# Start of a linear-attention and GEGLU kernel: fills of two load buffers moved ahead, first batch's casts, kv, x and norms regrouped by head pairs, first two gate tiles run by rows of x

## The chip, the cores and the metric

The kernel runs on one core of a Trainium2 chip. The metric is the device time of one execution in microseconds (us). The page of a profile counts from the first to the last record of the core; that span is some 2 us shorter than the time of the same execution. Where a difference matters the number of runs and a standard error stand beside it.

## The reference, cut to what matters

```python
# q, k, v: 8 batches x 8 heads x 576 rows x 64, f32; moe_w_*: 512 x 1536 (out: 1536 x 512)
q_s = softmax(q, axis=-1)                       # over the 64 columns of a head
k_s = softmax(k, axis=2)                        # over the 576 rows
kv  = einsum('bhsd,bhse->bhde', k_s, v)         # 64 x 64 for each head
x   = einsum('bhsd,bhde->bhse', q_s, kv)        # -> (4608, 512) rows
out = (gelu(x @ w_gate) * (x @ w_val)) @ w_out
```

## The kernel before

All large work is matmuls in f16. Two heads share the 128 rows of a weight tile ("a head pair", `hp` 0 to 3; "a group" is two pairs). PSUM is the memory that matmuls write to. `xt` holds x transposed; "row i of x" is the part of it that comes from head pair i. "A gate tile" is 128 of the 1536 columns of w_gate and w_val: four matmuls for each of the two (`psg` and `psv`), one for each row of x. Before the first gate matmul the first batch has to go through: load q, exponential on ScalarE, row sums, reciprocal and multiply on VectorE or GpSimd, transposes on TensorE (to `eqt`); load k, exponential; load v, cast to f16; kv on TensorE, its norm on VectorE (`kv_sb`); x on TensorE, copied to f16 (`xt`). While TensorE has nothing to do it multiplies a tile of zeros (`warm_pe`, the warm-ups); in the profile before, these matmuls start 0.43 us apart at first and 0.22 us apart later.

```python
    for nm, n, fill in (("k", 2, -1e30), ("v", 1, 0.0), ("q", 2, 0.0)):   # after the other memsets
        for i in range(n):
            t = const.tile([P, H, NC * D], f32, name=f"{nm}t{i}")
            (nc.vector if i == 0 else nc.gpsimd).memset(t[:, :, 0:D], fill)
    ...
    def norm_sum(b, hp, n0=0):         # one head pair
        ...
        nc.vector.reduce_sum(rq, e, axis=mybir.AxisListType.X)
        nc.vector.reciprocal(out=rrq, in_=rq)
    def norm_mul(b, hp, eng="dve"):    # VectorE, or GpSimd with eng="pool"
        ...
    def unit_kv(b, g):                 # two head pairs in one PSUM tile
        pskv = ps_att.tile([P, 2, 2 * VW], f32, name="pskv", tag="att")
        for j in range(2): ...         # 5 matmuls each
        nc.vector.reciprocal(out=rck, in_=pskv[:, :, D])
        for j in range(2): ...         # kv_sb = pskv * rck * mask
    ...
    exp("q", 0, 0, 4, 1); exp("q", 0, 4, 8, 1); exp("k", 0, 0, 4); exp("k", 0, 4, 8)
    warm_pe(35)
    norm(0, 0, "dve", 1);  norm(0, 1, "pool", 1)
    norm(0, 2, "dve", 1);  norm(0, 3, "pool", 1)
    unit_t(0, 0, "dve")                # transposes of pairs 0, 1, and the copy to eqt
    warm_pe(9)
    cast_v(0, 0, 4, "dve")             # heads 0-3 in one instruction
    cast_v(0, 4, 6, "act")
    unit_t(0, 1, "act")
    cast_v(0, 6, 8, "dve")
    ...
    warm_pe(2)
    unit_kv(0, 0)
    unit_kv(0, 1)
    unit_x(0, 0, "act", True);  unit_x(0, 1, "act", True)
    unit_x(0, 2, "dve", True);  unit_x(0, 3, "act", True)
    ...
    # ffn_first: psg, psv of gate tile 0 with rows 0, 1 of x, then of tile 1,
    # then row 2 of both, then row 3 of both
```

The softmax here doesn't subtract the row's maximum and nothing guards it: scores larger than these inputs give would overflow.

Of the kernel before, what the change touches and what calls it, by code (L numbers as in the profile page):

```python
# [9 lines left out]
f32 = mybir.dt.float32  # L10
# [8 lines left out]
def kernel(  # L19
# [44 lines left out]
    warm = const.tile([P, 512], f16)  # L64
    nc.vector.memset(warm, 0.0)
    ident = const.tile([P, P], f16)
    make_identity(nc, ident)
    mask = const.tile([P, 2, D], f32)
    nc.vector.memset(mask, 0.0)
    nc.vector.memset(mask[0:64, 0, :], 1.0)  # L70
    nc.vector.memset(mask[64:128, 1, :], 1.0)
    tiny = const.tile([P, 80], f32)
    nc.vector.memset(tiny, 0.0)
    ek_b, eq_b, v16_b = [], [], []
    for i in range(2):
        ek_b.append(const.tile([P, NC, C], f16, name=f"ek{i}"))
        eq_b.append(const.tile([P, NC, C], f16, name=f"eq{i}"))
        v16_i = const.tile([P, NC, H, VW + 1], f16, name=f"v16_{i}")
        nc.gpsimd.memset(v16_i[:, :, :, D:D + 1], 1.0)
        v16_b.append(v16_i)  # L80
    xtr = const.tile([P, HP, B * REM], f16)
    q0r = const.tile([64, H, D], f32)
    eq0r = const.tile([P, C], f16)
    nc.vector.memset(eq0r[64:128, :], 1.0)

    ld_b = {}
    for nm, n, fill in (("k", 2, -1e30), ("v", 1, 0.0), ("q", 2, 0.0)):
        ld_b[nm] = []
        for i in range(n):
            t = const.tile([P, H, NC * D], f32, name=f"{nm}t{i}")  # L90
            (nc.vector if i == 0 else nc.gpsimd).memset(t[:, :, 0:D], fill)
            ld_b[nm].append(t)

# [67 lines left out]
    def norm_sum(b, hp, n0=0):  # L161
# [6 lines left out]
        st[(b, "norm", hp)] = (e, rrq, n)  # L168

    def norm_mul(b, hp, eng="dve"):  # L170
        e, rrq, n = st[(b, "norm", hp)]
        (nc.gpsimd if eng == "pool" else nc.vector).tensor_tensor(  # L172
            out=e, in0=e, in1=rrq.unsqueeze(-1).to_broadcast((P, n, 2, D)), op=ALU.mult)
# [19 lines left out]

    def unit_kv(b, g):
        pskv = ps_att.tile([P, 2, 2 * VW], f32, name="pskv", tag="att")
        for j in range(2):
            hp = 2 * g + j
            for n in range(NC):
                nc.tensor.matmul(  # L199
                    pskv[:, j, :], ek_b[b % 2][:, n, hp * P:(hp + 1) * P],  # L200
                    v16_b[b % 2][:, n, 2 * hp:2 * hp + 2, 0:VW],
                    start=(n == 0), stop=(n == NC - 1))
        rck = att.tile([P, 2], f32, name="rck", tag="rck")
        nc.vector.reciprocal(out=rck, in_=pskv[:, :, D])
        for j in range(2):
            kv_sb = att.tile([P, 2, D], f16, name="kv_sb", tag="kv", bufs=12)
            nc.vector.scalar_tensor_tensor(  # L207
                out=kv_sb,
                in0=pskv[:, j, :].rearrange("p (h e) -> p h e", e=VW)[:, :, 0:D],
                scalar=rck[:, j:j + 1], in1=mask, op0=ALU.mult, op1=ALU.mult)  # L210
            st[(b, "kv", 2 * g + j)] = kv_sb

    def get_eqt(b):
# [5 lines left out]
    def unit_t(b, g, eng="dve"):  # L219
        eqt = get_eqt(b)  # L220
        pst = ps_att.tile([P, 2, MAIN], f16, name="pst", tag="att")
        for j in range(2):
            hp = 2 * g + j
            for n in range(NM):
                nc.tensor.transpose(  # L225
                    pst[:, j, n * P:(n + 1) * P],
                    eq_b[b % 2][:, n + 1, hp * P:(hp + 1) * P], ident)
        copy_on(eng, eqt[:, 2 * g:2 * g + 2, 0:MAIN], pst)

# [56 lines left out]
    def unit_xrem(b, eng="act"):  # L286
# [4 lines left out]
        copy_on(eng, xtr[:, :, b * REM:(b + 1) * REM], psx)  # L291

    def warm_pe(n):
        ps = ps_big.tile([P, 512], f32, name="pswarm", tag="mm")
        for _ in range(n):
            nc.tensor.matmul(ps, ident, warm, start=True, stop=True)  # L296
# [25 lines left out]
    def ffn_first(xt, after):  # L322
# [14 lines left out]
        for fi, (psg, psv) in enumerate(ps):  # L337
            mm_gv(psg, wg_sb, xt, fi, [3])
            mm_gv(psv, wv_sb, xt, fi, [3])
            hts.append(gate(psg, psv))  # L340
        return hts

# [80 lines left out]
    exp("k", 0, 4, 8)  # L423
    warm_pe(35)
    norm(0, 0, "dve", 1)
    norm(0, 1, "pool", 1)
    norm(0, 2, "dve", 1)
    norm(0, 3, "pool", 1)
    unit_t(0, 0, "dve")
    warm_pe(9)  # L430
    cast_v(0, 0, 4, "dve")
    cast_v(0, 4, 6, "act")
    unit_t(0, 1, "act")
    cast_v(0, 6, 8, "dve")
    for h0 in (0, 4):
# [4 lines left out]
    warm_pe(2)  # L440
    unit_kv(0, 0)
    unit_kv(0, 1)
    cast_w("wg", 0, "pool")
    cast_w("wv", 0, "pool")
    unit_x(0, 0, "act", True)
    unit_x(0, 1, "act", True)
    unit_x(0, 2, "dve", True)
    unit_x(0, 3, "act", True)
    preload(ACTF.Gelu)
# [10 lines left out]
    def at(b, kind, i, *fns):  # L460
# [3 lines left out]

    at(0, FI, NFI - 1, L(exp, "q", 1), L(exp, "k", 1, 0, 4),
       L(cast_w_o, 3), L(cast_w_o, 4), L(cast_w_o, 5),
       L(norm, 1, 0), L(norm, 1, 1, "pool"), L(norm_sum, 1, 2), L(norm_mul, 1, 2, "pool"),
       L(cast_v, 1, 0, 4, "act"), L(exp, "k", 1, 4, 8))
# [6 lines left out]
              [L(unit_x, 1, 3, "dve")]]  # L475
    first = {0: [[], []], 1: first1}

# [53 lines left out]
    for b in order:  # L531
        xt = get_xt(b) if b < B else xtr
        hts = []
        fi0 = 0
        if b in first:
            hts = ffn_first(xt, first[b])
            fi0 = len(hts)
            ride(b, FI, fi0 - 1)
# [57 lines left out]
```

## Time and profile before

| | before |
|---|---|
| median of the runs before the prediction | 321.93 us (3 runs, 321.76 to 321.95) |
| span of the profiled execution | 319.8 us |
| TensorE busy | 314.4 us (98%) |
| q of the first batch lands (ScalarE's first exponential) | 6.44 us |
| k, v land | 10.07, 13.03 us |
| first kv matmul | 14.60 us |
| third gate tile starts | 20.78 us |

How to read it: TensorE is the bound, and it runs without a gap from the first gate tiles to the end except for a few short waits. The landing of a load is read here as the start of the first ScalarE instruction that needs it. The chain of waits gives a first kv matmul at 14.66 where the timeline has 14.60, since the chain cuts at the end of the matmul before; I use the timeline.

### The profile page before, as it was taken

Reading aid. Unit: us, or ns where it says so; the run is one execution under the profiler, and the core shown is the slowest. Engines: PE = TensorE matmul, PEld = TensorE weight load, DVE = VectorE, ACT = ScalarE, POOL = GpSimd, SP = SyncE. Lnnn points to the kernel's source line nnn. Section 1 sums busy time; section 2 is a strip of 40 time slices with the busy share of each in tenths; the row PEclk is TensorE's granted clock in tenths of the full one; section 3 lists DMA queues with packets and bytes.
Section 4 is the critical chain, followed back from the end, with each engine's and each line's share of the span. In section 5 each row is a group of like instructions: output and inputs, shape, how many; then the busy total and the mean of one; then the engine's idle time right before and its main releaser. Section 6 shows DMA issues by size and latency. Waiting matters only on the chain.

```text
span 319.8 us, 4482 instructions
## 1 busy us (share of the span) xinstructions
PE 314.4 (98%) x1650; PEld 149.5 (47%) x1650; DVE 194.7 (61%) x343; ACT 140.0 (44%) x178; POOL 44.5 (14%) x60
## 2 busy tenths in 40 slices
PE   8999999999999999999999999999999999999995
PEld 3544454445445444544444444444444444444443
DVE  3944366498889578846794679457952444233431
ACT  3563564898352563246423743384321233103300
POOL 2567460340002000120003000300000000000000
PEclk9999999999999999999999999999999999999999
DMA  6999999940187216821492039302011110040002
GB/s 230 367 383 395 400 389 385 394 148 0 68 291 250 54 66 210 321 62 66 124 383 81 29 124 373 121 21 119 14 55 29 68 66 0 16 108 10 0 34 99
DMA packets 42342, 50.76 MB, mean 159 GB/s; under 512 B 3408, under 2 KB 38096, under 8 KB 42320
## 3 DMA queue, kind: packets, MB, share of 16 engines
q1 hardware_dynamic: 42176, 50.41, 45.6%
q8 instruction: 13, 0.21, 0.3%
q14 instruction: 9, 0.07, 0.1%
q10 hardware_dynamic: 144, 0.07, 0.1%
HBM read 37.75 MB, written 9.44 MB: 148 GB/s over the span
## 4 chain that ended last, share of the span: by engine, by line
PE 96%; ACT 1%; issue 1%; DVE 1%; POOL 0%; POOLq 0%; ACTq 0%
PE psg L304 28%; PE psy L348 28%; PE psv L304 28%; PE pswarm L296 4%; PE pskv L199 3%; PE psx L282 2%; PE pst L225 1%; PE psl L369 1%; DVE kv_sb L207 0%; ACT L309 0%; ACT L148 0%; PE psxr L289 0%; ACT eq L148 0%; PE pstr L237 0%; ACT gl L309 0%
## 5 line engine op out<-in xcount | busy, mean ns | idle before, releaser
L309 ACT ACTIVATE gl<-psg 128x512 f32<-128x512 f32 x108 | 63.9, 598 | 127.3 <-PE psg L304 125.5
L311 DVE SCALAR_TENSOR_TENSOR ht<-psv,gl 128x512 f16<-128x512 f32 x108 | 72.9, 682 | 64.7 <-PE psv L304 63.2
L304 PE MATMUL psg<-xt,wg_sb 128*128 128x512 f16 x384 | 100.6, 379 | 0.2
L304 PE MATMUL psv<-xt,wv_sb 128*128 128x512 f16 x384 | 100.2, 379 | 0.0
L348 PE MATMUL psy<-wo_sb,ht 128*128 128x512 f16 x420 | 95.5, 379 | 0.0
L304 PEld LDWEIGHTS <-wv_sb 128*128 128x128 f16 x432 | 42.2, 98 | 51.5 <-issue 0.9
L304 PEld LDWEIGHTS <-wg_sb 128*128 128x128 f16 x432 | 41.5, 98 | 47.6 <-issue 0.8
L348 PEld LDWEIGHTS <-ht 128*128 128x128 f16 x420 | 40.4, 98 | 47.2 <-DVE ht L311 0.2
L397 DVE TENSOR_SCALAR yo<-psy 128x512 f32<-128x512 f32 x30 | 20.6, 689 | 31.0 <-PE psy L348 31.0
L126 POOL CAST v<-vt 128x640 f16<-128x640 f32 x26 | 18.3, 743 | 140.1 <-DMA vt<-in_v_dram 122.9
L165 DVE TENSOR_REDUCE rq<-eq 128x10 f32<-128x640 f16 (+1 forms) x32 | 25.4, 792 | 9.3 <-ACT eq L148 8.9
L172 DVE TENSOR_TENSOR eq<-eq,rrq 128x640 f16<-128x640 f16 (+1 forms) x28 | 22.9, 817 | 0.3
L148 ACT ACTIVATE ek<-kt 128x1280 f16<-128x1280 f32 (+1 forms) x11 | 19.1, 1746 | 3.0 <-DVE rrq L167 1.6
L148 ACT ACTIVATE eq<-qt 128x2560 f16<-128x2560 f32 (+1 forms) x9 | 18.3, 2049 | 4.3 <-DMA qt<-in_q_dram 4.2
L248 DVE STREAM_TRANSPOSE et<-eq 128x640 f16<-128x640 f16 x20 | 16.9, 845 | 0.7
L128 ACT CAST xt<-psx 128x512 f16<-128x512 f32 x17 | 9.2, 588 | 15.9 <-PE psx L282 15.9
L296 PE MATMUL pswarm<-warm,ident 128*128 128x512 f16 x46 | 12.3, 430 | 1.4 <-POOL ident masks.py:199 1.4
L304 PE MATMUL psg<-xtr,wg_sb 128*128 128x512 f16 x48 | 12.3, 379 | 0.0
L304 PE MATMUL psv<-xtr,wv_sb 128*128 128x512 f16 x48 | 12.3, 379 | 0.0
L199 PEld LDWEIGHTS <-ek 128*128 128x128 f16 x160 | 10.3, 97 | 3.6 <-issue 0.4
L199 PE MATMUL pskv<-v,ek 128*128 128x130 f16 x160 | 11.8, 220 | 0.0
L130 DVE CAST xt<-psx 128x512 f16<-128x512 f32 x15 | 9.7, 682 | 1.8 <-PE psx L282 1.8
(59 smaller groups left out, 129.4 us busy)
## 6 DMA issues: line engine op xcount, KB each, us to landing
out_dram<-yo SPq DMA_DIRECT2D x14, 512.0 KB, 3.5
qt<-in_q_dram SPq DMA_DIRECT2D x9, 512.0 KB, 6.7
kt<-in_k_dram SPq DMA_DIRECT2D x7, 640.0 KB, 7.4
vt<-in_v_dram SPq DMA_DIRECT2D x7, 640.0 KB, 7.9
qt<-in_q_dram SPq DMA_DIRECT2D x7, 640.0 KB, 6.1
kt<-in_k_dram SPq DMA_DIRECT2D x7, 512.0 KB, 8.0
vt<-in_v_dram SPq DMA_DIRECT2D x7, 512.0 KB, 8.5
eqt<-et SPq DMA_DIRECT2D x80, 40.0 KB, 1.9
```

The lines of the kernel that those rows point to most:

```text
L126: nc.gpsimd.tensor_copy(out=dst, in_=src)
L148: nc.scalar.activation(out=dst[:, n0:NC, h0 * D:h1 * D].rearrange("p n (h d) -> p h n d", d=D), in_=tiles[(nm, b)][:, h0:h1, n0 * D:NC * D ...
L165: nc.vector.reduce_sum(rq, e, axis=mybir.AxisListType.X)
L172: (nc.gpsimd if eng == "pool" else nc.vector).tensor_tensor(out=e, in0=e, in1=rrq.unsqueeze(-1).to_broadcast((P, n, 2, D)), op=ALU.mult)
L199: nc.tensor.matmul(pskv[:, j, :], ek_b[b % 2][:, n, hp * P:(hp + 1) * P], v16_b[b % 2][:, n, 2 * hp:2 * hp + 2, 0:VW], start=(n == 0), sto ...
L248: nc.vector.transpose(out=et[:, :, hp].rearrange("p c (n i) -> p n c i", i=32), in_=eq_b[b % 2][:, :, hp * P:(hp + 1) * P].rearrange("p n ...
L296: nc.tensor.matmul(ps, ident, warm, start=True, stop=True)
L304: nc.tensor.matmul(ps, w[:, ci, fi * P:(fi + 1) * P], xt[:, ci, :], start=(ci == 0), stop=(ci == HP - 1))
L309: nc.scalar.activation(out=gl, in_=psg, func=ACTF.Gelu)
L311: nc.vector.scalar_tensor_tensor(out=ht, in0=psv, scalar=_H_SCALE, in1=gl, op0=ALU.mult, op1=ALU.mult)
L348: nc.tensor.matmul(psy, hts[fi][:, ns * P:(ns + 1) * P], wo_sb[:, fi, :], start=(fi == 0), stop=(fi == NFI - 1))
L397: nc.vector.tensor_scalar(out=yo, in0=psy, scalar1=1.0 / _H_SCALE, scalar2=None, op0=ALU.mult)
```

## The change

The intent is to shorten the stretch up to 20.78 us. It puts the fills of k's and v's load buffers ahead of the other memsets, so that the load of k can be issued sooner; sums the rows of q for two head pairs with one instruction and gives one more multiply to VectorE; drops two warm-ups; casts v by head pair on two engines; does kv of heads 0 to 3 first and x of those heads before the rest; and runs the first two gate tiles row of x by row of x, with x of the upper heads in between. In the second batch, q's exponential is split and one multiply moves from GpSimd to VectorE.

```diff
     nc.vector.memset(warm, 0.0)
+    nc.vector.memset(ld_b["k"][0][:, :, 0:D], -1e30)      # fills of the load buffers: before, the last memsets
+    nc.vector.memset(ld_b["v"][0][:, :, 0:D], 0.0)
     nc.vector.memset(tiny, 0.0)
     nc.vector.memset(mask, 0.0)
 ... (cut: tiles are allocated earlier, the same memsets follow; norm_pair, kv_mm, kv_norm are new functions)
-    warm_pe(35)
-    norm(0, 0, "dve", 1)
-    norm(0, 1, "pool", 1)
-    norm(0, 2, "dve", 1)
-    norm(0, 3, "pool", 1)
-    unit_t(0, 0, "dve")
+    norm_pair(0, 0, 1, ("dve", "dve"))
+    warm_pe(33)
+    unit_t(0, 0, None)
+    evac_t0 = st["evac_t"]
+    norm_pair(0, 1, 1, ("dve", "pool"))
+    evac_t0("dve")
     warm_pe(9)
-    cast_v(0, 0, 4, "dve")
+    unit_t(0, 1, None)
+    cast_v(0, 0, 2, "dve")
+    cast_v(0, 2, 4, "act")
+    cast_v(0, 6, 8, "dve")
     cast_v(0, 4, 6, "act")
-    unit_t(0, 1, "act")
-    cast_v(0, 6, 8, "dve")
 ... (cut: loads)
     warm_pe(2)
-    unit_kv(0, 0)
-    unit_kv(0, 1)
+    kv_mm(0, 0, 0)
+    kv_mm(0, 0, 1)
+    kv_norm(0, 0)
+    kv_mm(0, 1, 1)
     unit_x(0, 0, "act", True)
+    kv_mm(0, 1, 0)
     unit_x(0, 1, "act", True)
-    unit_x(0, 2, "dve", True)
-    unit_x(0, 3, "act", True)
+    st["evac_t"]("dve")
+    kv_norm(0, 1)
 ... (cut: ffn_first0, for batch 0 alone)
+        go(0, (0, 1))          # gate tile 0, rows 0 and 1 of x: psg, psv of a row, then of the next
+        xs()                   # x of pairs 2 and 3
+        go(1, (0, 1))
+        go(0, (2,))
+        go(1, (2,))            # then row 3 of tile 0, its gelu; row 3 of tile 1, its gelu
 ... (cut)
-    at(0, FI, NFI - 1, L(exp, "q", 1), L(exp, "k", 1, 0, 4),
+    at(0, FI, NFI - 1, L(exp, "q", 1, 0, 4), L(exp, "q", 1, 4, 8), L(exp, "k", 1, 0, 4),
-       L(norm, 1, 0), L(norm, 1, 1, "pool"), L(norm_sum, 1, 2), L(norm_mul, 1, 2, "pool"),
+       L(norm, 1, 0), L(norm, 1, 1), L(norm_sum, 1, 2), L(norm_mul, 1, 2, "pool"),
```

More of the change, by code (lines that the diff above doesn't have):

```diff
@@ L64 @@
     warm = const.tile([P, 512], f16)
-    nc.vector.memset(warm, 0.0)
     ident = const.tile([P, P], f16)
-    make_identity(nc, ident)
     mask = const.tile([P, 2, D], f32)
-    nc.vector.memset(mask, 0.0)
-    nc.vector.memset(mask[0:64, 0, :], 1.0)
-    nc.vector.memset(mask[64:128, 1, :], 1.0)
     tiny = const.tile([P, 80], f32)
-    nc.vector.memset(tiny, 0.0)
     ek_b, eq_b, v16_b = [], [], []
@@ L77 @@
         eq_b.append(const.tile([P, NC, C], f16, name=f"eq{i}"))
-        v16_i = const.tile([P, NC, H, VW + 1], f16, name=f"v16_{i}")
-        nc.gpsimd.memset(v16_i[:, :, :, D:D + 1], 1.0)
-        v16_b.append(v16_i)
+        v16_b.append(const.tile([P, NC, H, VW + 1], f16, name=f"v16_{i}"))
     xtr = const.tile([P, HP, B * REM], f16)
@@ L83 @@
     eq0r = const.tile([P, C], f16)
-    nc.vector.memset(eq0r[64:128, :], 1.0)
-    ld_b = {}
-    for nm, n, fill in (("k", 2, -1e30), ("v", 1, 0.0), ("q", 2, 0.0)):
-        ld_b[nm] = []
-        for i in range(n):
-            t = const.tile([P, H, NC * D], f32, name=f"{nm}t{i}")
-            (nc.vector if i == 0 else nc.gpsimd).memset(t[:, :, 0:D], fill)
-            ld_b[nm].append(t)
+    ld_b = {nm: [const.tile([P, H, NC * D], f32, name=f"{nm}t{i}") for i in range(n)]
+            for nm, n in (("k", 2), ("v", 1), ("q", 2))}
+    nc.vector.memset(warm, 0.0)
+    nc.vector.memset(ld_b["k"][0][:, :, 0:D], -1e30)
+    nc.vector.memset(ld_b["v"][0][:, :, 0:D], 0.0)
+    nc.vector.memset(tiny, 0.0)
+    nc.vector.memset(mask, 0.0)
+    nc.vector.memset(mask[0:64, 0, :], 1.0)
+    nc.vector.memset(mask[64:128, 1, :], 1.0)
+    nc.vector.memset(eq0r[64:128, :], 1.0)
+    nc.vector.memset(ld_b["q"][0][:, :, 0:D], 0.0)
+    make_identity(nc, ident)
+    for i in range(2):
+        nc.gpsimd.memset(v16_b[i][:, :, :, D:D + 1], 1.0)
+    nc.gpsimd.memset(ld_b["k"][1][:, :, 0:D], -1e30)
+    nc.gpsimd.memset(ld_b["q"][1][:, :, 0:D], 0.0)
     wg_sb = wpool.tile([P, HP, F], f16, name="wg_sb")
@@ L168, in norm_sum, with norm_pair @@
         st[(b, "norm", hp)] = (e, rrq, n)
+    def norm_pair(b, g, n0, engs):
+        n = NC - n0
+        e = eq_b[b % 2][:, n0:NC, 2 * g * P:(2 * g + 2) * P].rearrange("p n (h d) -> p n h d", d=D)
+        rq = att.tile([P, n, 4], f32, name="rq2", tag="rq2", bufs=2)
+        nc.vector.reduce_sum(rq, e, axis=mybir.AxisListType.X)
+        rrq = att.tile([P, n, 4], f32, name="rrq2", tag="rrq2", bufs=2)
+        nc.vector.reciprocal(out=rrq, in_=rq)
+        for j, eng in enumerate(engs):
+            st[(b, "norm", 2 * g + j)] = (e[:, :, 2 * j:2 * j + 2], rrq[:, :, 2 * j:2 * j + 2], n)
+            norm_mul(b, 2 * g + j, eng)
     def norm_mul(b, hp, eng="dve"):
@@ L192, with kv_mm, kv_norm @@
     st = {}
-    def unit_kv(b, g):
-        pskv = ps_att.tile([P, 2, 2 * VW], f32, name="pskv", tag="att")
-        for j in range(2):
-            hp = 2 * g + j
-            for n in range(NC):
-                nc.tensor.matmul(
-                    pskv[:, j, :], ek_b[b % 2][:, n, hp * P:(hp + 1) * P],
-                    v16_b[b % 2][:, n, 2 * hp:2 * hp + 2, 0:VW],
-                    start=(n == 0), stop=(n == NC - 1))
+    def kv_mm(b, g, j):
+        if (b, "pskv", g) not in st:
+            pool, tag = (ps_big, "mm") if (b, g) == (0, 1) else (ps_att, "att")
+            st[(b, "pskv", g)] = pool.tile([P, 2, 2 * VW], f32, name="pskv", tag=tag)
+        hp = 2 * g + j
+        for n in range(NC):
+            nc.tensor.matmul(
+                st[(b, "pskv", g)][:, j, :], ek_b[b % 2][:, n, hp * P:(hp + 1) * P],
+                v16_b[b % 2][:, n, 2 * hp:2 * hp + 2, 0:VW],
+                start=(n == 0), stop=(n == NC - 1))
+    def kv_norm(b, g):
+        pskv = st[(b, "pskv", g)]
         rck = att.tile([P, 2], f32, name="rck", tag="rck")
@@ L211, in unit_kv @@
             st[(b, "kv", 2 * g + j)] = kv_sb
+    def unit_kv(b, g):
+        kv_mm(b, g, 0)
+        kv_mm(b, g, 1)
+        kv_norm(b, g)
     def get_eqt(b):
@@ L227, in unit_t @@
                     eq_b[b % 2][:, n + 1, hp * P:(hp + 1) * P], ident)
-        copy_on(eng, eqt[:, 2 * g:2 * g + 2, 0:MAIN], pst)
+        st["evac_t"] = lambda eng: copy_on(eng, eqt[:, 2 * g:2 * g + 2, 0:MAIN], pst)
+        if eng:
+            st["evac_t"](eng)
     def unit_trem(b):
@@ L291, in unit_xrem @@
         copy_on(eng, xtr[:, :, b * REM:(b + 1) * REM], psx)
+    pswarm = ps_big.tile([P, 512], f32, name="pswarm", tag="mm")
     def warm_pe(n):
-        ps = ps_big.tile([P, 512], f32, name="pswarm", tag="mm")
+        ps = pswarm
         for _ in range(n):
@@ L340, in ffn_first, with ffn_first0, go @@
             hts.append(gate(psg, psv))
+        return hts
+    def ffn_first0(xt, xs):
+        ps = {}
+        for fi in range(2):
+            for nm in ("g", "v"):
+                ps[(nm, fi)] = ps_big.tile([P, 512], f32, name="ps" + nm, tag="mm")
+        def go(fi, cis):
+            for ci in cis:
+                mm_gv(ps[("g", fi)], wg_sb, xt, fi, [ci])
+                mm_gv(ps[("v", fi)], wv_sb, xt, fi, [ci])
+        go(0, (0, 1))
[3 more added lines that the diff above has]
+        go(1, (2,))
+        hts = []
+        for fi in range(2):
+            go(fi, (3,))
+            hts.append(gate(ps[("g", fi)], ps[("v", fi)]))
         return hts
@@ L475, with x_upper @@
               [L(unit_x, 1, 3, "dve")]]
-    first = {0: [[], []], 1: first1}
+    def x_upper():
+        unit_x(0, 2, "dve")
+        unit_x(0, 3, "act")
     at(1, FI, 2, L(unit_trem, 1))
@@ L534 @@
         fi0 = 0
-        if b in first:
-            hts = ffn_first(xt, first[b])
+        if b < 2:
+            hts = ffn_first0(xt, x_upper) if b == 0 else ffn_first(xt, first1)
             fi0 = len(hts)
```

## The prediction

> **What bounds the kernel now.** I read the page first: busy shares, then the chain that ended last, then that chain in order of time, the timeline of the first 21 us, and the DMA share by stretch.
>
> ```profile
> PE 314.4 (98%) x1650; PEld 149.5 (47%) x1650; DVE 194.7 (61%) x343; ACT 140.0 (44%) x178; POOL 44.5 (14%) x60
> ...
> PE 96%; ACT 1%; issue 1%; DVE 1%; POOL 0%; POOLq 0%; ACTq 0%
> ```
>
> TensorE is the bound over the whole span (319.8 us), its clock is granted in full in all 40 slices, and a 512-column matmul leaves every 0.2155 us (36 psy matmuls in 7.77 us of chain). Only the start, where TensorE does filler or waits, can be shortened without removing matmuls. The chain in order of time shows that start:
>
> ```profile
> 1.36 9.65 PE pswarm L296 x35
> ...
> 11.66 1.94 PE pswarm L296 x9
> ...
> 14.23 0.43 PE pswarm L296 x2
> 14.66 0.69 PE pskv L199 x10
> 15.38 0.18 DVE rck L204
> ...
> 15.58 0.61 DVE kv_sb L207 x2
> ...
> 16.31 0.36 DVE kv_sb L207
> ...
> 16.72 0.65 PE psx L282 x2
> 17.36 0.56 PE psg L304 x2
> ```
>
> Up to 14.66 TensorE only warms up and transposes; then the chain is kv, its norm on VectorE, x, and the gates. The timeline shows what the first gate matmuls wait for:
>
> ```profile
> 13.03 0.73 ACT L128 CAST v<-vt 128x640 f16<-128x640 f32 x1 [0.54 <-DMA vt<-in_v_dram]
> 13.06 2.21 DVE L130 CAST v<-vt 128x1280 f16<-128x1280 f32 x2
> ...
> 15.99 1.37 PE L282 MATMUL psx<-eqt,kv_sb 128*128 128x512 f16 x4
> ...
> 16.42 1.57 ACT L128 CAST xt<-psx 128x512 f16<-128x512 f32 x3 [1.14 <-PE psx L282]
> ...
> 17.20 0.72 PE L304 MATMUL psg<-xt,wg_sb 128*128 128x512 f16 x2
> ...
> 17.76 0.59 PE L304 MATMUL psv<-xt,wv_sb 128*128 128x512 f16 x2
> ...
> 20.78 1.03 PE L304 MATMUL psg<-xt,wg_sb 128*128 128x512 f16 x4
> ```
>
> The second psg matmul starts at 17.54 (17.76 less one step), just as the second x copy on ScalarE ends (16.42 + one step of 0.53 + 0.59). From 17.54 TensorE runs without a gap: 15 matmuls of 0.2155 are 3.23 us, which gives 20.77, and the third gate tile does start at 20.78. So **the time at which the third gate tile starts, 20.78, is the number to follow**: what it moves, the end moves, provided no new wait appears later.
>
> The DMA view by stretch says when the data comes:
>
> ```profile
> 3.50:4.00 0.50, 0.50 (x3) 0.23 (x2) 0.44 (x2) 0.00 (x0) 0.00 (x0) 1.00 1.06 369
> ...
> 6.00:6.50 0.50, 0.50 (x4) 0.20 (x2) 0.00 (x0) 0.06 (x1) 0.00 (x0) 1.00 1.04 371
> ```
>
> Its last two columns are the DMA share and GB/s. From 3.5 us on the engines are full at about 370 to 390 GB/s. q (two 512 KB transfers) lands at 6.4, k at 10.0 (3.8 + 6.2 to landing), v at 12.9 (5.1 + 7.8): in order of issue and one behind the other.
>
> **What the Trainium skill says.** (1) "TensorE: Matmul & The Clock Gate", "Wait — 56ns, not 53.3ns?": 512-column matmuls follow each other at 426.7 ns cold and 215.7 ns warm; the trace agrees (weight loads of the first warm-ups are 0.43 apart, later matmuls 0.2155). (2) "VectorE: DVE Perf Modes", "The perf-mode tier table": tensor_reduce has only the 1x mode. The trace agrees: 512 elements 0.69 us, 640 elements 0.82, so 1.02 ns an element and only some 0.17 fixed; joining two sums saves little. (3) "ScalarE: Activation LUTs", "What ACT_TABLE_LOAD costs": 1283 ns for the load, and another 1380 ns of drain. The trace has 1.28, but the next activation follows 0.02 later, so I count 1.28 alone. (4) "DMA: Bandwidth & Descriptors", "Queues, rings and completion order": descriptors of one ring are consumed in order. The landings above agree.
>
> **The change part by part.**
>
> *Memsets reordered.* The k load waited for its fill on VectorE and was issued at 3.12; with the fill second on the engine it is ready near 1.6, and the load can go out when q's issues end, at 2.20: 0.9 us earlier. But the engines are full before k's bytes would begin, with no dip at 6.4 where q ends and k follows. Worth: 0.
>
> *Norms by two pairs.* VectorE, start to start: sum of 1024 elements 0.69 + 512 x 1.02 ns = 1.21 (1.24 with the gap), reciprocal 0.24, multiplies 0.61 each. From 7.53 (first half of q's exponentials): reciprocal 8.77, multiplies 9.00 and 9.61 (done 10.24), second sum 10.22, reciprocal 11.46, multiply 11.70 beside GpSimd's (11.7 + 1.04 = 12.75; before 13.77). With GpSimd sharing, that multiply takes 0.84 as before, so the copy of the first transposes starts at 12.54, before 12.51. VectorE gains nothing; what is gained is that both transposes wait for no GpSimd multiply.
>
> *Two warm-ups less:* 0.43 us of TensorE, on the path. 33 end at 10.58, when the first two heads' pairs are ready (10.24). Transposes 0.62, 9 warm-ups 1.94: 13.14. Transposes 0.62 (inputs ready 12.75), 2 warm-ups 0.43: **kv may start at 14.19, before 14.66.**
>
> *Casts by head pair.* v lands at 12.95 at best; VectorE casts heads 0-1 from 13.06 to 13.8 (640 elements at the rate of 1280 in 1.40 is 0.73), ScalarE heads 2-3 to 13.76. Before, heads 0-3 were whole at 14.46, nearly as late as the warm-ups; this is what permits the smaller filler. kv for two pairs ends 14.19 + 0.69 = 14.88.
>
> *kv, its norm and x.* VectorE's other cast ends at about 14.7, so the reciprocal is at 14.92 and the two kv_sb at 15.12 and 15.42. TensorE does kv of pair 3 meanwhile (0.32, to 15.2), waits, and issues x0 at 15.52 (0.1 after the kv_sb ends; before 15.99). kv of pair 2 fills 15.73 to 16.05, then x1 16.05. ScalarE starts its copies 0.43 after x: 15.95 and 16.48, done 16.54 and 17.07.
>
> *Rows of x first.* psg and psv with row 0 at 16.54 and 16.76, row 1 from **17.07**. From there TensorE has 14 gate matmuls and x2, x3: 16 x 0.2155 = 3.45, so the third gate tile starts at **20.52, 0.26 before 20.78**. Moving x2, x3 and five kv matmuls (0.75 of work) does not remove them; they fill waits, but about 0.35 (before x0), 0.27 (before row 0) and 0.1 (before row 1) stay idle.
> Checks on that stretch: the copy of x2 (VectorE, 17.9 to 18.6) is needed at about 18.8; that of x3 stands behind the gelu table (17.07 + 1.28 + 0.2 = 18.55, copy to 19.15) and is needed at 19.7. PSUM buffers: pswarm and pskv are long free when tile 1 takes them. The first weight cast starts when its data lands (13.7), so it is not earlier, but is done by 15.7, before 16.5. None of these shows.
>
> *Second batch.* The exponential in two halves (two of 1.26 for one of 2.34, ScalarE +0.18) gives the first sums 1.1 us earlier; the second multiply goes from GpSimd (done near 46.0) to VectorE (done near 44.3). The transposes at 45.81 took 0.52 instead of 0.45, so about 0.07 comes off; output copies start 0.2 earlier and wait for nothing. The stalls on kv_sb and eqt near 49 and 53 stay.
>
> Sum: 0.26 + 0.07 = 0.33, up to 0.1 more if TensorE meets its data slightly better. I take 0.38: **321.93 - 0.38 = 321.55.**
>
> **The rivals.** *A: the gain vanishes.* v's landing at 12.95 fixes the chain; if GpSimd slows VectorE's casts (the second one took 0.89 for 640 elements beside GpSimd's cast), or the eqt copy now on VectorE between the two kv norms delays x2, TensorE waits where it warmed up. For it: the chain has at most 0.3 us of play. Against it: the first cast ends before the weights land at 13.7. It would give 321.9. *B: earlier data.* If the early k issue closes gaps in the queue, v lands up to 0.9 earlier. Against it: the full DMA share from 3.5; and TensorE's 44 warm-ups would still hold kv at 14.19, so no more than about 0.15 beyond mine: 321.3 to 321.4. *C: new waits.* More gate tiles open before the first gelu, with table load and x3 in one ScalarE queue; if x3 came 1 us late, the gain would be eaten and 322.4 result. There is half a us of slack against it. *D: the fills were worth more*, TensorE idle nowhere: 0.26 + 0.7 = 1.0 off, 320.9; the kv_sb dependency speaks against it.
>
> **Range and chances.** The movable part is the stretch from 10.6 to 20.8 plus about 0.1 in the second batch; the runs before lie within 0.2. A and the good end of B and D set 321.0 to 322.0. Two per cent is 6.4 us, six times the whole movable waiting, so faster 0.01, within 0.98, slower 0.01.
>
> **What would show it.** In the changed profile: k and v landing as before (10.0, 12.9) though k is issued near 2.2; the kv matmuls beginning near 14.2; x0 near 15.5; row 1 gates near 17.1 and the third gate tile near 20.5, released by matmuls, not by ScalarE. A v cast starting much before 13.0 would prove the memset step wrong; a TensorE wait between 17.1 and 20.5 would prove the slack checks wrong; a shift at the end of the span that differs from the shift of the third tile by over 0.2 would mean the second batch was misjudged.

## The result, and the profile after

| | before | after |
|---|---|---|
| median of 5 runs each, same chip | 321.93 us (321.76 to 322.07) | 322.08 us (321.64 to 322.69) |
| ratio | | 1.0005 (95%: 0.999 to 1.002) |
| span of the profiled execution | 319.8 us | 320.3 us |
| q, k, v land | 6.44, 10.07, 13.03 | 6.95, 10.43, 13.40 us |
| first kv matmul | 14.60 | 14.65 us |
| third gate tile | 20.78 | 21.05 us |

A ratio is the mean time of one kernel's fast runs over the mean of the other's of the same rounds, so it is not quite the ratio of the medians quoted. The two are the same within 2%, as predicted. But the time, 322.08, lies just above the range of 321.0 to 322.0, and nothing of the 0.38 us that was to be won is seen.

The page of the profile after, first the busy line, then the shares of the chain that ended last:

```profile
PE 313.7 (98%) x1648; PEld 149.2 (47%) x1648; DVE 196.2 (61%) x342; ACT 139.7 (44%) x179; POOL 42.7 (13%) x58
...
PE 90%; DVE 3%; ACT 2%; DMA 2%; issue 2%; POOL 0%; SPq 0%; ACTq 0%; DVEq 0%; POOLq 0%
```

TensorE has two matmuls less. But its share of the chain fell from 96% to 90%, and DMA is now in the chain with 2%. Before, the chain that is printed runs through the warm-ups, though by little: the 35 ended at 11.01 (1.36 + 9.65), and GpSimd's multiply, for which the second half of the first transposes waits too, at 11.21 (10.17 + 1.04). So q's chain was already level with the filler. Now q's chain alone carries the start. In order of time (start, duration, engine, what; "DMA" is a load until it lands):

```profile
1.56 5.30 DMA qt<-in_q_dram
6.95 1.06 ACT eq L148
8.04 1.23 DVE rq L175
9.30 0.26 DVE rrq L177
9.58 1.29 DVE eq L184 x2
10.88 1.14 DVE rq L175
12.04 0.26 DVE rrq L177
12.45 1.49 POOL eq L184
13.98 0.40 PE pst L246 x4
...
14.81 0.59 PE pskv L212 x10
15.43 0.18 DVE rck L220
15.63 0.36 DVE kv_sb L223
16.04 0.40 PE psx L305
...
21.22 0.86 PE psg L329 x4
```

From the landing of q there is no play left: exponential, sum, reciprocal, multiply, sum, reciprocal, a multiply on GpSimd, transposes, kv, norm, x, gates. So every tenth that q is late is a tenth at the third tile. And q is late: its first load lasts to 6.86, and the exponential starts at 6.95. Before, it started at 6.44:

```profile
6.44 2.00 ACT L148 ACTIVATE eq<-qt 128x1024 f16<-128x1024 f32 x2 [4.20 <-DMA qt<-in_q_dram]
```

What is different about q? Its loads are issued as before, at 0.73; what is new is that k's loads go out earlier, and v's behind them (3.59 instead of 4.44). The timeline of the kernel before, then of the changed one, SyncE's issues (start, duration, engine):

```profile
3.12 1.28 SPq L104 DMA_DIRECT2D kt<-in_k_dram  x2
```

```profile
2.24 1.31 SPq L104 DMA_DIRECT2D kt<-in_k_dram  x2
```

The DMA view of both kernels for 5.5 to 7 us, the stretch in which q ends; the first line is the busy share of the DMA engines in tenths in 40 slices of the stretch, the other has packets, bytes and the mean rate. Before, then after:

```profile
DMA  9989999889998998999999989999999799999999
...
DMA packets 483, 0.56 MB, mean 376 GB/s; under 512 B 16, under 2 KB 483, under 8 KB 483
```

```profile
DMA  9999999996989697766694959658979989699799
...
DMA packets 394, 0.45 MB, mean 298 GB/s; under 512 B 16, under 2 KB 394, under 8 KB 394
```

Before, the engines are busy nearly throughout. After, 14 of the 40 slices, all from 5.8 us on, have shares of only 4 to 7 tenths (before, one has), and the same queue moves 0.11 MB less in these 1.5 us. That is the first suspect, and the experiments below test it.

A sum for the two profiles. Third tile: 21.05 − 20.78 = +0.27, of which q is +0.51 and the rest, from q to the third tile, −0.24 (14.34 before, 14.10 after). After the third tile one wait differs: near 71 us TensorE waits for an `ht` of VectorE, 0.41 us in the changed kernel and 0.14 before, +0.27. The rest is −0.07. Together +0.47; the spans differ by 0.48.

The wait near 71 us, in the timelines before and after:

```profile
68.54 3.31 POOL L126 CAST v<-vt 128x640 f16<-128x640 f32 x4 [7.54 <-PE psv L304]
...
69.09 0.85 DVE L172 TENSOR_TENSOR eq<-eq,rrq 128x640 f16<-128x640 f16 x1
```

```profile
69.02 3.31 POOL L126 CAST v<-vt 128x640 f16<-128x640 f32 x4 [7.50 <-DMA vt<-in_v_dram]
...
69.22 1.19 DVE L184 TENSOR_TENSOR eq<-eq,rrq 128x640 f16<-128x640 f16 x1
...
71.06 1.02 PE L329 MATMUL psg<-xt,wg_sb 128*128 128x512 f16 x4 [0.25 <-DVE ht L336]
```

(The line's 0.25 counts from the modelled end of the transpose before; from start to start the matmul comes 0.41 us later than its step.) VectorE's multiply took 1.19 us instead of 0.85, and the `ht` behind it was late. This is in code that the change does not touch. Over all profiles the wait lies between 0 and 0.55 us, in both kernels (before: 0.14 and 0.32; the changed kernel unaltered: 0.41, 0.48 and 0), so it is scatter and not the change. The traces show what goes with it: how far into a cast on GpSimd the multiply begins. In four of these five profiles it began 0.55, 0.37, 0.20 and 0.13 us after a cast of 0.72 us had begun and took 0.85, 1.03, 1.19 and 1.26 us; in the fifth it began 0.16 us before the cast, took 0.82, and the cast took 1.25. What moves the cast against the multiply from one execution to the next is not shown.

### The profile page after: what moved, and what is told of

Same layout as the page of the kernel before. It is cut to its first block, busy times and chain, and to the rows that moved or that the text cites. A ratio compares the mean times of both kernels' runs of the same rounds, so it can differ in the third digit from the quotient of the medians.

```text
span 320.3 us, 4471 instructions
## 1 busy us (share of the span) xinstructions
PE 313.7 (98%) x1648; PEld 149.2 (47%) x1648; DVE 196.2 (61%) x342; ACT 139.7 (44%) x179; POOL 42.7 (13%) x58
## 4 chain that ended last, share of the span: by engine, by line
PE 90%; DVE 3%; ACT 2%; DMA 2%; issue 2%; POOL 0%; SPq 0%; ACTq 0%; DVEq 0%; POOLq 0%
PE psy L396 28%; PE psg L329 28%; PE psv L329 27%; PE pskv L212 3%; PE psx L305 2%; DMA qt<-in_q_dram 2%; PE psl L417 1%; DVE rq L175 1%; DVE ht L336 1%; ACT eq L148 1%; POOL eq L184 0%; DVE rq L165 0%; DVE eq L184 0%; PE pst L246 0%; ACT L334 0%
## 5 line engine op out<-in xcount | busy, mean ns | idle before, releaser
L165 DVE TENSOR_REDUCE rq<-eq 128x10 f32<-128x640 f16 x28 | 22.7, 811 | 4.9 <-ACT eq L148 4.5
L184 DVE TENSOR_TENSOR eq<-eq,rrq 128x640 f16<-128x640 f16 (+1 forms) x30 | 24.7, 827 | 0.3
L148 ACT ACTIVATE eq<-qt 128x2560 f16<-128x2560 f32 (+2 forms) x10 | 18.4, 1863 | 4.5 <-DMA qt<-in_q_dram 4.4
```

What stands on the lines that cost most here:

```text
L148: nc.scalar.activation(out=dst[:, n0:NC, h0 * D:h1 * D].rearrange("p n (h d) -> p h n d", d=D), in_=tiles[(nm, b)][:, h0:h1, n0 * D:NC * D ...
L184: (nc.gpsimd if eng == "pool" else nc.vector).tensor_tensor(out=e, in0=e, in1=rrq.unsqueeze(-1).to_broadcast((P, n, 2, D)), op=ALU.mult)
```

## The experiments

Sixteen runs were made, in four calls; those of one call were on one chip and share its runs of the kernel before. Two kernels that differ in one edit are called twins. In what follows "late k" is a kernel that issues k's load at 2.9 us or later, "early k" one that issues it at 2.2; v's load follows at 4.2 to 4.5 in the first and at 3.6 in the second, and no run moves one without the other. The landing times of k and v scatter from one execution to the next by more than most effects here (k 10.0 to 12.2, v 13.0 to 15.3), so one profile's start is read by its differences: kv against q, or kv against v.

My theory after the result: the early issue of k slows q's end, and the chain from q has no play. Rivals: the changed kernel is no worse and the result was scatter; a part of the change (norms, warm-ups, row order, second batch) is the loss.

### The changed kernel again, and the kernel before again

No edit.

> The changed kernel once more. If q's late landing (6.9 us in its first profile, 6.4 before) is an accident of that execution, this profile has q near 6.4 to 6.5, the third gate tile near 20.6 and a time near 321.6. If it belongs to the change, q lands near 6.9 again with a dip of the DMA rate between 5.8 and 6.8, and the third gate tile is near 21.0. Either way the times spread over about 1 us, against 0.3 for the kernel before.

> The changed kernel a third time, on the same chip as its late-k twin. By the same theory: 1.38 to 1.46 MB by 7 us with a dip, q near 6.7, third tile 14.1 after q, and a median 0.1 to 0.3 above the twin's.

> The kernel before once more, for a second profile on the same chip as the next three. If its start hangs on q's landing as strictly as the changed kernel's does, the third gate tile starts 14.3 us after q's first exponential (20.78 - 6.44 in the first profile), and the wait of TensorE near 70.6 us is about 0.14 again. If that first profile was lucky, the wait is 0.3 to 0.5 as in the changed kernel.

Measured: 321.81 us (5 runs) against 322.13 (11 runs of the kernel before), ratio 0.9992 (0.998 to 1.0004); the second time 321.75 (6 runs) against 322.07, ratio 0.9997 (0.9984 to 1.0011). With the five runs of the result the changed kernel has 16 runs with a mean of 321.94 ± 0.10. The kernel before has 42 runs with a mean of 322.01 ± 0.04. So the difference is −0.07 ± 0.11: the one result was a little unlucky (the mean of the 16 runs lies inside the predicted range), but the predicted −0.38 is not there. The three profiles agree on the chain: kv starts at q + 7.70, 7.69 and 7.68, and the third tile at q + 14.10, 14.10 and 14.09; the kernel before has q + 8.16 and 8.17, and q + 14.34 twice. So from q's landing the change is 0.24 us better each time, and q lands later each time (6.95, 6.69, 6.71 against 6.44 and 6.41).

### Is it k's early issue?

The changed kernel with the two fills put back behind the others:

```diff
     nc.vector.memset(warm, 0.0)
-    nc.vector.memset(ld_b["k"][0][:, :, 0:D], -1e30)
-    nc.vector.memset(ld_b["v"][0][:, :, 0:D], 0.0)
     ... (cut)
     nc.vector.memset(eq0r[64:128, :], 1.0)
+    nc.vector.memset(ld_b["k"][0][:, :, 0:D], -1e30)
+    nc.vector.memset(ld_b["v"][0][:, :, 0:D], 0.0)
```

> The changed kernel with k's and v's fills last again, so that k is issued near 3.1 instead of 2.2. If the early k load is what delays q (theory 1), q lands near 6.4 as before, kv starts near 14.3, and the time is 0.3 to 0.5 below the changed kernel's, near 321.6. If the landing is chance or the norms are the cause (theory 2), it stays within 0.15 of the changed kernel.

> The changed kernel with k's fill late, a second time. If the early k load is what slows the queue between 5.5 and 7 us (all seven profiles with it have moved 1.38 to 1.45 MB by 7 us, the three without it 1.50 to 1.55), this one has moved over 1.48 MB by 7 us, without a dip, and q lands by 6.6. If the three were luck, it can show the dip too.

And the other way round, the early fills alone in the kernel before (the edit is the one above in reverse):

> The kernel before with k's and v's fills first, so that k is issued near 2.2. Theory 1: q lands near 6.9 and the time rises by 0.2 to 0.4, to about 322.2, with a wider spread. Theory 2: no change, 321.9 within 0.1.

Measured: the late k gave 321.50 us, ratio 0.9982 (0.997 to 0.9994), and when run again 321.92, ratio 0.9994 (0.9982 to 1.0006). Against the unaltered changed kernel the means differ by 321.87 − 321.55 = 0.32 and 321.88 − 321.79 = 0.09; in the second pair the medians lie the other way round (321.75 early, 321.92 late). The DMA view of the late k for 5.5 to 7 us:

```profile
DMA packets 478, 0.57 MB, mean 378 GB/s; under 512 B 15, under 2 KB 478, under 8 KB 478
```

The rate is that of the kernel before again. The kernel before with the early k has a rate of 293 GB/s, and q at 6.71 instead of 6.44 or 6.41. Its first transposes then waited 0.47 us for GpSimd's multiply, and its last two warm-ups began at 14.33 instead of 14.07, so q's delay is on the path there too. Its time does not show the expected 0.2 to 0.4 us: 321.96 (6 runs, one at 323.82), ratio 1.0003 (0.9984 to 1.0022); the mean is 0.08 ± 0.34 above the kernel before of the same call, and 0.24 below it without the slowest run. That is too coarse to speak for or against. Its profile fell on that slowest run, with k at 12.19 and v at 15.29, so its later part says nothing.

This held in every profile: nine with an early k had 293 to 334 GB/s in this stretch, nine with a late k had 350 to 383. The mean landing of q was 6.71 against 6.49, 0.22 ± 0.06 later. The queue does not make this good: by 13 us the early ones had moved 3.53 to 3.68 MB and the late ones 3.68 to 3.77, on average 0.12 MB apart, which at 376 GB/s is, as an estimate, 0.3 us. k and v landed 0.34 ± 0.24 and 0.37 ± 0.25 later on average, so the loss need not come through q alone. The second profile of the late k shows the other bound: there v landed at 13.89, and kv started when v's cast was done, at v + 0.64. The chain of waits:

```profile
4.91 8.88 DMA vt<-in_v_dram
13.89 0.51 DVE v L130
14.53 0.75 PE pskv L212 x10
```

So kv waits for the later of q + 7.69 and v + 0.64, provided that the warm-ups are over. Late k is the better choice for the first and does not make the second worse, as far as these landings can tell.

### Do the two warm-ups matter?

```diff
-    warm_pe(33)
+    warm_pe(35)
```

> The changed kernel with 35 warm-ups again. If q's landing and the norms set the start, the two warm-ups cost nothing or at most 0.3 us, the less the later q lands: no difference for q after 6.9. If the filler sets it, as the prediction had it, the third tile is a full 0.43 us later whatever q does.

Measured: 321.76 us, ratio 0.9998 (0.9986 to 1.0011); kv at q + 7.69 and the third tile at q + 14.09, as without the edit. The chain of waits:

```profile
9.92 1.29 PE pswarm L321 x6
11.22 0.45 PE pst L246 x8
...
14.51 0.59 PE pskv L212 x10
```

From the 35 warm-ups to kv TensorE waits for nothing, so they are on the chain. They end level with q's chain: q landed at 6.66, and kv started at 14.35, which is q + 7.69. So dropping two is worth nothing in this execution, by a tie. In others it depends on when the step between the warm-ups falls from 0.43 to 0.22 us: over the profiles, 33 warm-ups took 8.59 to 10.16 us and 35 took 9.47 to 10.17.

### The norms

Each pair's norm by itself, as before, in the changed kernel:

```diff
-    norm_pair(0, 0, 1, ("dve", "dve"))
+    norm(0, 0, "dve", 1)
+    norm(0, 1, "pool", 1)
     ... (cut)
-    norm_pair(0, 1, 1, ("dve", "pool"))
+    norm(0, 2, "dve", 1)
+    norm(0, 3, "pool", 1)
```

> The changed kernel with the four norms of one head pair each, as before, GpSimd multiplying pairs 1 and 3. Theory 2 (the joined norms put the last multiply on GpSimd beside one on VectorE, 1.48 us instead of 1.04, and hold the second transposes by 0.44): the time falls by 0.2 to 0.4. Theory 1: the multiply of pair 3 is no earlier, since it follows q, and the time stays within 0.15 of the changed kernel.

Measured: 322.18 us, ratio 1.0001 (0.9988 to 1.0014), a mean of 322.16 against 321.87 for the changed kernel. That is 0.28 ± 0.10 us slower, where one theory had expected 0.2 to 0.4 faster and the other no change. In its profile the first transposes waited 0.95 us for GpSimd's multiply, and from there the chain stays on TensorE to the two warm-ups, which began at 14.21; two steps of 0.22 later, at 14.64 or q + 8.04, kv could have started. v landed at 14.04 and held it a little longer, to 14.70. So the norms by two pairs are worth 0.35 us or more at kv in this order: the pair's multiply on VectorE is what lets the first transposes go, and kv at q + 8.16 (before) against q + 7.69 comes with it.

And the norms and casts by pairs alone, in the kernel before:

```diff
-    norm(0, 0, "dve", 1); norm(0, 1, "pool", 1); norm(0, 2, "dve", 1); norm(0, 3, "pool", 1)
+    norm_pair(0, 0, 1, ("dve", "dve"))
+    norm_pair(0, 1, 1, ("dve", "pool"))
     ... (cut)
-    cast_v(0, 0, 4, "dve")
+    cast_v(0, 0, 2, "dve")
+    cast_v(0, 2, 4, "act")
```

> The kernel before with only the joined norms and the casts of v by head pair; 35 warm-ups, fills, kv, x and gates as before. Theory A (the whole gain in the start comes from these two; the row order and the split kv lose 0.2 of it again, since after kv the changed kernel takes 6.41 us to the third gate tile and the kernel before 6.18): kv starts 7.7 us after q's exponential, the third gate tile 13.9 after it, and the time is 0.4 below before. Theory B (the row order is what gains): third tile at 14.3 or later after q.

Measured: 322.82 us, ratio 1.0028 (1.0015 to 1.0041), the slowest kernel, and a miss of mine. The chain of waits:

```profile
15.62 0.62 DVE kv_sb L219 x2
16.24 0.14 issue
16.37 0.75 PE pskv L211 x10
```

The kv matmuls of the second group start only at 16.37, and the trace puts this down to the `kv_sb` of the first group, done at 16.24. In the kernel before they start at 15.33, just after ScalarE's copy to `eqt` (14.27 to 15.28). My edit put a second cast in front of that copy, but here too it was over at 15.64. So the second group probably waited for the PSUM buffer of the first, one of two in that pool; why it got that one is not shown. Either way the run does not test what it was meant to test. In the change that kv tile comes from another PSUM pool and the copy is on VectorE, so the casts by pair cannot be judged without these two lines. Also, here the 35 warm-ups did bind: kv started at 14.63 though q + 7.69 would have been 14.11.

### The row order

The old order of the first gate tiles, with x of all four pairs ahead of it, in the changed kernel:

```diff
+            if b == 0:
+                x_upper()
-            hts = ffn_first0(xt, x_upper) if b == 0 else ffn_first(xt, first1)
+            hts = ffn_first(xt, [[], []] if b == 0 else first1)
```

> The changed kernel with the upper pairs' x before all gates, and the first two tiles in the old order. If the row order is what gains in the start, the third gate tile starts 14.35 to 14.5 us after q's exponential instead of 14.10, and the time is 0.25 to 0.4 above the changed kernel. If the start hangs on something else, it stays at 14.1.

Measured: 322.22 us, ratio 1.0007 (0.9995 to 1.002). From the first kv matmul to the third tile it took 6.66 us, 0.25 more than the 6.41 of the changed kernel. (Only this stretch is to be compared: the 33 warm-ups took 10.16 us in this profile and held kv to q + 7.98.) The chain of waits:

```profile
16.22 0.59 DVE eqt L130
16.94 0.36 DVE kv_sb L223
17.35 0.65 PE psx L305 x2
```

The `eqt` copy stands on VectorE between the two kv norms, and x of pairs 2 and 3 waits for both; with the old order, the gates wait too. So a fair test of the row order needs that copy out of the way. The second kernel does that, on the late k:

```diff
     warm_pe(2)
+    st["evac_t"]("dve")
     kv_mm(0, 0, 0); kv_mm(0, 0, 1); kv_norm(0, 0)
+    kv_mm(0, 1, 0); kv_mm(0, 1, 1); kv_norm(0, 1)
     ... (cut: unit_x of pairs 0 to 3 one after the other, and ffn_first in the old order)
```

> Late k fill, joined norms and casts by pair as in the change, but kv of all pairs in a row, the second transposes' copy ahead of kv's norms, all x ahead of the gates and the first two tiles in the old order. Theory A (row order and split kv gain nothing over this order, since the chain kv, kv_sb, x0, two ScalarE copies holds row 1 either way): the third gate tile comes 6.2 us after kv's start, as in the kernel before, against 6.41 in the change, and the time is 0.1 to 0.3 below the late-k kernel. Theory B (the row order hides work that otherwise stands in the way): 6.5 or more after kv.

Measured: 321.58 us, ratio 0.999 (0.9976 to 1.0003). From kv to the third tile it took 6.18 us, as in the kernel before and 0.23 less than with the rows; the times do not separate it from the late k (means 321.56 ± 0.15 and 321.67 ± 0.10). The chain of waits, in which v is the bound:

```profile
4.92 8.56 DMA vt<-in_v_dram
13.58 0.90 DVE v L130 x2
14.47 0.60 DVE eqt L130
...
16.38 0.65 PE psx L305 x2
...
20.61 0.86 PE psg L329 x4
```

So the new order of kv, x and rows gains nothing by itself over the straight order with an early copy. The prediction had this too (6.33 by its own steps against 6.18 of the kernel before), and the measured 6.41 is 0.08 above it.

### The second batch

```diff
-    at(0, FI, NFI - 1, L(exp, "q", 1, 0, 4), L(exp, "q", 1, 4, 8), L(exp, "k", 1, 0, 4),
+    at(0, FI, NFI - 1, L(exp, "q", 1), L(exp, "k", 1, 0, 4),
-       L(norm, 1, 0), L(norm, 1, 1), ...
+       L(norm, 1, 0), L(norm, 1, 1, "pool"), ...
```

> The changed kernel with the second batch's exponential in one piece and its second multiply on GpSimd, as before. The prediction: 0.07 us slower at the transposes near 46 us, nothing else. The rival: the second batch's change brought the longer wait near 70.6 us (0.33 to 0.48 against 0.14), and without it that wait is 0.14 and the kernel is 0.2 faster.

> The late-k kernel with separate reciprocals, and the second batch's exponential and multiply as before the change. If the second batch's change is worth 0.07 as predicted, or nothing, this is within 0.15 of its twin without it (rck_again). If it costs, as the mean of the earlier run without it hinted (321.52 against 321.94), this is 0.2 to 0.4 faster than the twin.

Measured: 321.74 us in the changed kernel, ratio 0.9988 (0.9976 to 1.0001), and its profile has 0.55 us of the wait near 71 us. A rival was that the moved second batch causes this wait; it falls, since the wait is there with the old second batch. In the best kernel (next section) the old second batch gave 321.30, ratio 0.9988 (0.9974 to 1.0002), a mean of 321.50 against 321.42 of its twin. Its profile has a wait of 0.22 us at the transposes at 45.9 us; that of the first has none there. The times cannot tell, even the sign: in the best kernel the old form is 0.08 ± 0.28 slower, in the changed kernel it has a mean of 321.52, 0.42 ± 0.19 faster than all 16 runs of the changed kernel. The predicted 0.07 is neither shown nor refuted.

### A version that beats both

The stretch from kv to x has a wait of 0.36 us in the changed kernel, because one reciprocal serves two head pairs, so the norm of the first pair waits for the matmuls of the second. Each of pairs 0 and 1 gets its own PSUM tile and its own reciprocal, on the late k:

```diff
+    def kv_one(b, hp, big):
+        ps = (ps_big if big else ps_att).tile([P, 2 * VW], f32, name="pskv", tag="mm" if big else "att")
+        ... (cut: 5 matmuls, reciprocal of column D, kv_sb)
-    kv_mm(0, 0, 0)
-    kv_mm(0, 0, 1)
-    kv_norm(0, 0)
+    kv_one(0, 0, False)
+    kv_one(0, 1, True)
```

> The changed kernel with k's fill late, and the kv norm of pairs 0 and 1 each with its own PSUM tile and reciprocal, so that pair 0's kv_sb need not wait for pair 1's matmuls. If the chain kv, kv_sb, x, ScalarE copy is what holds the gates, x0 starts 0.3 us earlier after kv and the third tile comes 13.75 to 13.85 us after q's exponential; time 0.25 below the late-k kernel. If something else holds them (weights, second copy), 14.1.

> The kernel with late k fill and one reciprocal each for pairs 0 and 1, again, beside its early-k twin. Expected 321.2 to 321.6, third gate tile 13.8 after q's exponential unless v lands later than q + 7.1, over 1.48 MB moved by 7 us.

And the same with the fills first, as a second test of the early k:

> The same kernel with the fills of k and v first, as in the change. If the early k load costs time and not only bytes, its mean is 0.15 to 0.4 above the twin's and under 1.46 MB have moved by 7 us. If the fills' order is worth nothing in time, as the prediction had it, the means differ by less than 0.15.

Measured: 321.23 us (6 runs, 320.89 to 322.19), ratio 0.9981 (0.9969 to 0.9994), and on another chip 321.44 (5 runs), ratio 0.9989 (0.9975 to 1.0002). The 11 runs have a mean of 321.40 ± 0.13, 0.6 us or 0.19% below the kernel before and 0.27 ± 0.16 below the late k without this edit. The stretch shows it more clearly: from kv to the third tile all four kernels with the edit take 6.11 or 6.12 us, against 6.40 or 6.41. The chain of waits of the second one:

```profile
14.26 0.30 PE pskv L232 x5
14.58 0.18 DVE rck L237
14.79 0.36 DVE kv_sb L239
15.19 0.40 PE psx L320
20.37 0.86 PE psg L344 x4
```

Only five kv matmuls stand ahead of the reciprocal, where the changed kernel had ten. The twin with the early k took 321.91, ratio 0.9998 (0.9986 to 1.0011); the means are 321.85 ± 0.06 and 321.42 ± 0.17, so the early fills cost 0.42 ± 0.18 us. The DMA view for 5.5 to 7 us has 362 GB/s for the late k and 295 for the early one.

All that differs between these kernels is the place of two memsets. That the early issue slows the queue at q's end is shown, by 18 profiles without an overlap. That the kernel pays for it rests on three pairs of twins (0.32 ± 0.12, 0.09 ± 0.27 and 0.42 ± 0.18 by the same reckoning), on average 0.28 ± 0.11: likely, though no single pair would do. How much of it goes through q and how much through v is not separated. In the profile of this early twin v was late (14.39) and held kv to v + 0.66, at 15.05, where q + 7.69 would have been 14.59.

What stays open is why the queue slows. The busy share of the engines dips in the stretch, as shown above, but whether k's or v's requests get in the way of q's, and where, no run here shows.

## Why the prediction was wrong, step by step

**The step that failed is "Memsets reordered. … Worth: 0."** The argument was that full DMA engines cannot be filled more, so an earlier issue changes nothing. The issue did move as worked out (2.24), and k did not land earlier (10.43). But the earlier issue made things worse: 298 instead of 376 GB/s while q was ending, and q 0.22 us later on average, 0.51 in the profiled execution. In time it cost about 0.3 us (0.28 ± 0.11 over three pairs of twins), which is most of the expected 0.38. With the fills put back, the rest of the change comes close to the predicted size, though not by all of the predicted steps: 10 runs of the late k have a mean of 321.67 ± 0.10, 0.34 ± 0.11 below the kernel before.

**The rivals.** Rival A came nearest in size ("the gain vanishes", 321.9), but for another reason: neither VectorE's casts nor the `eqt` copy took the gain. Rival B had the sign wrong, since it took an earlier issue to be harmless at worst. I had listed no rival in which a load becomes slower, although the change issued one earlier. C and D fell: TensorE runs without a gap from 17.60 to 21.05.

**Norms by two pairs.** The joined sum was right, 1.22 us against 1.21. The multiply on GpSimd was not. The prediction took 1.04 us from the row before. It measured 1.48, since in the new order VectorE starts its own multiply first. Two lines of the timeline before, then of the one after:

```profile
10.17 1.04 POOL L172 TENSOR_TENSOR eq<-eq,rrq 128x512 f16<-128x512 f16 x1 [7.58 <-DVE rrq L167]
...
10.84 0.92 DVE L172 TENSOR_TENSOR eq<-eq,rrq 128x512 f16<-128x512 f16 x1
```

```profile
12.33 0.69 DVE L184 TENSOR_TENSOR eq<-eq,rrq 128x512 f16<-128x512 f16 x1
12.45 1.48 POOL L184 TENSOR_TENSOR eq<-eq,rrq 128x512 f16<-128x512 f16 x1 [9.85 <-DVE rrq L177]
...
13.98 0.40 PE L246 MATMUL pst<-ident,eq 128*128 128x128 f16 x4 [0.44 <-POOL eq L184]
```

Where GpSimd was first, VectorE's multiply was stretched to 0.92; where VectorE was first, it took its 0.69 and GpSimd's took 1.48. The second transposes then wait 0.44 us for GpSimd. The prediction said that both transposes would wait for no GpSimd multiply; one of them does. This used up the 0.39 us of play that the prediction had between those inputs (12.75) and the warm-ups (13.14), which is why a late q goes straight to the end.

**Two warm-ups less.** "0.43 us of TensorE, on the path" held only in part: putting them back changed nothing in the time, and in that profile they tied with q's chain; in one other kernel 35 of them did bind. The gain from q + 8.16 to q + 7.69 comes from the norms, with a shorter filler that mostly no longer stands in the way. The sum also took 0.62 us twice for eight transposes, from rows in which TensorE waited for GpSimd in the middle; without that wait they take 0.45 (chain of the 35 warm-ups). With 0.45 the filler would have let kv start at 13.85. The start predicted for kv, 14.19, would still have come out with q at 6.44 (6.44 + 7.69 = 14.13), but by luck: the transposes were taken too long and GpSimd's multiply too short.

**Casts.** ScalarE's two casts took 1.35, 0.67 for one, near the predicted 0.73. VectorE's two took 1.55 together in the profiled execution, where GpSimd was at work beside them, but 0.90 in the profiles in which GpSimd was mostly idle then (the chain of the straight order shows it), some 0.45 each, against 0.73 predicted from a row in which GpSimd worked too. Neither moved kv in the profiled execution: only the first cast on each engine is needed for it, and VectorE's second was done in time for the norm.

**kv, x and rows.** The stretch from kv to the third tile was 6.41 against 6.33, right to 0.08; the copies and the table load had the slack that was claimed. With q at 6.95 instead of 6.44 (+0.51), kv at q + 7.70 instead of q + 7.75 (14.19 − 6.44; −0.05) and this +0.08, the third tile is 0.54 above the predicted 20.52 by this sum; it was 21.05, 0.53 above.

**Second batch.** 0.07 was predicted, and the two profiles have −0.07 once the wait near 71 us is taken out. The times neither show nor refute it. The test that I gave, that the end must shift like the third tile within 0.2, was a bad one: the scatter of that one wait is larger.

**The range.** It took the scatter of the kernel before from three runs within 0.2 us. The changed kernel alone spread over 321.34 to 322.78 in 16 runs. Even for an unbiased prediction a range of ±0.5 around a median of five was narrow at its upper end.

## What to carry to other kernels

Issuing a load earlier need not be free, even when the queue is full: look at the rate in the stretch where the load ahead of it ends, since that one can be the one on the path. Before counting on a chain, ask how much play it has; where there is none, the scatter of a landing goes into the time in full, and single profiles mislead, so compare twins that differ in one line and read differences from the landing. A reciprocal or copy that serves two pieces makes the first wait for the second: splitting it took 0.30 us off the stretch from kv to the third tile (6.41 to 6.11), while the reordering of rows took nothing off the straight order's 6.18.

## What the Trainium skill lacked or had wrong

- "DMA: Bandwidth & Descriptors", "Queues, rings and completion order", says how descriptors of one ring are ordered, but not that loads issued earlier behind the first can slow the queue: 293 to 334 GB/s with k issued at 2.2 us and v at 3.6, 350 to 383 with k at 2.9 or later and v at 4.2 or later (nine profiles each). Nor does it say how far landings scatter with issue times unchanged: v from 13.1 to 15.3 us in the nine profiles with v issued at 3.6.
- "GPSIMD Engine Reference", "1. Specifications", says that GpSimd's SBUF interfaces are shared with VectorE, with contention for instructions with two SBUF inputs. The traces agree; the section has no size for it. In the pairs shown here the one that started second was stretched: 1.48 instead of 1.04 us on GpSimd, 0.92 instead of 0.69 on VectorE.
- "TensorE: Matmul & The Clock Gate", "Part 1: The HAM clock gate", says that the moment at which the clock comes up varies from run to run, in one place by ±500 ns, in another from 6 to 14 slow matmuls for the same kernel. The traces agree with the second: the first 6 to 14 warm-ups were 0.43 us apart, so the fast step came 2.5 to 5.9 us after the first (18 profiles), and ±500 ns is too little. The prediction should have used this: 33 warm-ups took 8.59 to 10.16 us.
- "VectorE: DVE Perf Modes", "The perf-mode tier table", was right where my row was not: it has f32 copies between SBUF tiles at twice the base rate, and a cast of 640 elements took some 0.45 us with GpSimd mostly idle. The row that I used was 1280 elements in 1.40 us beside GpSimd.
- "ScalarE: Activation LUTs", "What ACT_TABLE_LOAD costs", adds 1380 ns of drain to the 1283 ns of a table load. No trace here shows the drain: each of the 324 loads in 18 profiles took 1.28 us, and where nothing else held it the next activation followed 0.01 to 0.02 us later.
